# Crossbar transposes amid the loads, and token mixing pair by pair, in a fused sparse attention and MLP mixer

## The chip, the cores and the metric

The kernel runs on one core of one Trainium2 chip. The metric is device time in microseconds, the median over runs. A trace of one execution gives the span, which is 1.6 to 2.1 us shorter than the time of the same execution. PE is the matmul engine, PEld its weight loads, DVE the vector engine, ACT the scalar engine, POOL and SP the engines that here mostly issue DMAs: POOL the loads, SP the stores and the crossbar transposes. Executions of one kernel still differ by an us or two; in the record, those of the kernel before have a mean clock of 0.986 to 1.000, and those at 0.993 are mostly 0.7 to 1.5 us longer.

## The reference

Four batches of eight heads, 768 positions, 64 channels. Attention is masked by blocks of 32 (band, edges, three sampled blocks per row), then a token mixing with a residual and a channel mixing with a residual follow.

```python
scores = scale * np.matmul(q, k.transpose(0, 1, 3, 2))
scores = np.where(mask, scores, -1e9)
attn = softmax(scores);  x = attn @ v                       # to (B, S, H*D)
h = np.maximum(x.transpose(0, 2, 1) @ w_tok1, 0.0) @ w_tok2
u = x + h.transpose(0, 2, 1)
out = u + np.maximum(u @ w_ch1, 0.0) @ w_ch2
```

## The kernel before

Heads go in 16 pairs, nine steps each. A step is a block of scores on PE, its exp on ACT, from pair 4 on its masking on DVE, and its product with the values (PV) on PE. Before that, DVE lays a pair's keys and queries out anew (the relayout), and they are transposed: on PE with an evacuation (a copy of PE's result to where it is used), or by a DMA, the crossbar. A planner inside the kernel simulates the engines and decides, when the kernel is built, in which order each engine gets its instructions. On the chip every engine keeps the order it was given, and stands (waits with its next instruction) where the plan was wrong. What matters here:

```python
def landing(issue, nbytes):                     # the plan's idea of when a load lands
    dma["free"] = max(dma["free"], issue + 3.2 * US) + nbytes / RATE      # RATE = 200
    return Ev(dma["free"] + 0.15 * US)

def relayout(p):                                # DVE: loaded keys, queries -> order for the transpose
    ...
        lay = sbw.tile([128, NC, 2, D], BF16, tag=f"{nm}lay", bufs=2, name=f"{nm}lay{p}")
        nc.vector.tensor_copy(out=lay[...], in_=raw.rearrange("p h c d -> p c h d"))
    ...
    if nm != "v" and p >= 3:
        deps.append(qT_there[p - 2, 1])         # two buffers: the transpose of p-2 has read them
    if nm != "v" and p >= NPE:
        deps.append(all_loaded)                 # not before all loads are there

def crossbar(p):                                # pairs p >= NPE (8): transposed by DMA
    nc.sync.dma_start_transpose(out=bufs[p % NV][:, 0, :]..., in_=lays[nm]...)
    deps = [lays[nm + "ev"], mask_there, qk_done[p - NV]]
    ev = P.op(("sp",), {"sp": 900.0}, deps, emit, prio=1, lat=5000.0)     # planned landing: 5 us
```

Pairs below NPE are transposed on PE, 12 matmuls a pair, and evacuated by DVE or ACT. From pair 4 on the exps are masked on DVE by a multiplication ("cut"), scores run on 64 rows at a time, two steps per visit, and PE fills with channel mixing.

The softmax here doesn't subtract the row's maximum and nothing guards it: scores larger than these inputs give would overflow.

Of the kernel before, what the change touches and what calls it, by code (L numbers as in the profile page):

```python
# [8 lines left out]
FP32 = mybir.dt.float32  # L9
BF16 = mybir.dt.bfloat16  # L10
# [40 lines left out]
class Planner:  # L51
# [21 lines left out]
    def stream(self, prio, gen):  # L73
        self.streams.append([prio, self.count, gen, None])
        self.count += 1
        self.streams.sort(key=lambda s: (s[0], s[1]))
# [27 lines left out]
    def step(self):  # L104
# [3 lines left out]
        if self.free_at["pe"] <= self.now:  # L108
            for s in self.streams:
# [65 lines left out]
def kernel(  # L175
# [23 lines left out]
    NPE = 8  # L199
# [24 lines left out]
    RATE = 200.0  # L224

    def landing(issue, nbytes):
        dma["free"] = max(dma["free"], issue + 3.2 * US) + nbytes / RATE
        return Ev(dma["free"] + 0.15 * US)
# [62 lines left out]
    def first(eng, nm, src, hf):  # L291
        eng.dma_start(
            out=f32[nm][:, :, 3 * hf : 3 * hf + 3, :],
            in_=APx(src, 3 * hf * D, [[NC * D, 128], [S * D, 2], [1, 3 * D]]),
        )

    nc.sync.dma_start(out=samp64[R, :], in_=sampled_blocks)
    first(nc.scalar, "q", q, 0)
    first(nc.sync, "k", k, 0)
    first(nc.sync, "k", k, 1)  # L300
    first(nc.sync, "q", q, 1)

# [12 lines left out]
    def idle_mm():  # L315
        nc.tensor.matmul(
            out=idle_ps[:, 0, :], lhsT=free(one[:, 0:1], 0, [[0, 128]]),
            rhs=free(one[:, 0:1], 0, [[0, 512]]), start=True, stop=True,
        )

    for i in range(8):
        idle_mm()
# [17 lines left out]
    load_pair(2, 6.4 * US, 2)  # L340
    load_tok(8.7 * US)
    load_pair(3, 10.2 * US, 3)
# [26 lines left out]
    nc.vector.tensor_copy(out=sampf[R, :], in_=samp64[R, :].bitcast(I32))  # L369
# [10 lines left out]
    nc.vector.tensor_copy(out=ktb[0][R, 1, 0:384], in_=indf[:, 0:384])  # L380
# [5 lines left out]
    def first_lay(copy, nm, hf):  # L386
        copy(
            out=lay0[nm][:, 3 * hf : 3 * hf + 3, :, :],
            in_=f32[nm][:, :, 3 * hf : 3 * hf + 3, :].rearrange("p h c d -> p c h d"),
        )  # L390

    def first_turn(nm, hf):
        t = psM.tile([128, 3, 128], BF16, tag="pm", name=f"t{nm}first{hf}")
        for c in range(3):
            nc.tensor.matmul(
                out=t[:, c, :], lhsT=lay0[nm][:, 3 * hf + c, :, :].rearrange("p h d -> p (h d)"),
                rhs=ident[:, :], start=(c == 0), stop=(c == 2), is_transpose=True,
            )
        return t

    def first_evac(copy, nm, hf, hd, t):
        buf = (ktb if nm == "k" else qtb)[0]
        copy(
            out=buf[0:64, hd, 384 * hf : 384 * hf + 384],
            in_=t[64 * hd : 64 * hd + 64, :, :].rearrange("p c s -> p (c s)"),
        )

    def e2_mm(hf, pool, tag):
        t = pool.tile([128, 512], FP32, tag=tag, name=f"pm_e2_{hf}")
        nc.tensor.matmul(  # L410
            out=t[R, 0:384], lhsT=t2add[R, :], rhs=indf[:, 384 * hf : 384 * hf + 384],
            start=True, stop=True,
        )
        return t

    def e2_copy(copy, hf, hd, t):
        copy(out=qtb[0][R, hd, 384 * hf : 384 * hf + 384], in_=t[R, 0:384])

    vcopy, acopy = nc.vector.tensor_copy, nc.scalar.copy
    first_lay(acopy, "q", 0)  # L420
    qt0 = first_turn("q", 0)
    first_lay(acopy, "k", 0)
    kt0 = first_turn("k", 0)
    e2a, e2b = e2_mm(0, psM, "pm"), e2_mm(0, psO, "po")
    for i in range(4):
        idle_mm()
    first_evac(acopy, "q", 0, 0, qt0)
    first_evac(acopy, "q", 0, 1, qt0)
    e2_copy(acopy, 0, 0, e2a)
    first_evac(vcopy, "k", 0, 0, kt0)  # L430
    first_evac(vcopy, "k", 0, 1, kt0)
    e2_copy(vcopy, 0, 1, e2b)
    first_lay(acopy, "k", 1)
    first_lay(vcopy, "q", 1)
    START = 6.3 * US
# [3 lines left out]
    P.free_at["dve"] = START + 550.0  # L439
    f_there = {("k", 0): Ev(START), ("q", 0): Ev(START), ("k", 1): Ev(), ("q", 1): Ev()}  # L440

# [3 lines left out]

    def first_rest():

        def band(eng):
            nc.vector.tensor_copy(out=ktb[0][R, 1, 384:S], in_=indf[:, 384:S])

        P.op(("dve",), {"dve": 250.0}, [], band, prio=0)
        for nm in ("k", "q"):
            box, last, rel = {}, Ev(), Ev()

            def emit(nm=nm, box=box, rel=rel):
                P.take("pm", rel)
                box["t"] = first_turn(nm, 1)

            yield 330.0, [Ev(START + (200.0 if nm == "k" else 600.0))], [("pm", 1)], emit, last
            for hd in range(2):  # L460
                def evac(eng, nm=nm, hd=hd, box=box):
                    first_evac(vcopy, nm, 1, hd, box["t"])

                ev = P.op(("dve",), {"dve": 350.0}, [last], evac, prio=0)
                f_there[nm, 1].same_as = ev
                rel.same_as = ev
        box, last, rel = {}, Ev(), Ev()

        def emit():
            P.take("pm", rel)  # L470
            box["t"] = e2_mm(1, psM, "pm")

        yield 330.0, [], [("pm", 1)], emit, last
        for hd in range(2):
            def copy(eng, hd=hd, box=box):
                e2_copy(vcopy, 1, hd, box["t"])

            e2_there = P.op(("dve",), {"dve": 555.0}, [last], copy, prio=0)
            rel.same_as = e2_there
        rows_there[0] = e2_there  # L480
        built.add(("row", 0))
        for n in range(1, NV):
            def spread(eng, n=n):
# [6 lines left out]
                ("dve",) if n == 1 else ("sp",), {"dve": 560.0, "sp": 800.0}, [e2_there], spread,  # L490
# [10 lines left out]
    def mask_stream():  # L501
# [13 lines left out]
        yield 330.0, [rows_there[0]], [("pm", 1)], emit, last  # L515
# [36 lines left out]
    all_loaded = Ev()  # L552

    def relayout(p):
        lays = {}
        for nm in ("k", "q", "v") if p else ("v",):
# [18 lines left out]
            if nm != "v" and p >= NPE:  # L575
                deps.append(all_loaded)
            lays[nm + "ev"] = P.op(("dve",), {"dve": 320.0}, deps, emit, prio=2 if nm != "v" else 3)
# [4 lines left out]
    def crossbar(p):  # L582

        lays = relayout(p)
        for nm, bufs, there in (("k", ktb, kT_there), ("q", qtb, qT_there)):
# [6 lines left out]
            ev = P.op(("sp",), {"sp": 900.0}, deps, emit, prio=1, lat=5000.0)  # L592
            there[p, 0], there[p, 1] = ev, ev

    def transposes(p):
# [4 lines left out]
        if p == 0:  # L600
# [3 lines left out]
            for hd in range(2):  # L604
                kT_there[p, hd], qT_there[p, hd] = f_there["k", 1], f_there["q", 1]
# [5 lines left out]
        for nm, bufs, there in (("k", ktb, kT_there), ("q", qtb, qT_there)):  # L611
# [29 lines left out]
            for hd in range(2):  # L641
# [7 lines left out]
                ev = P.op(("dve", "act"), {"dve": 550.0, "act": 740.0}, [last], evac, prio=2)  # L649
# [4 lines left out]
    def alias(a, b):  # L654
        a.same_as = b

# [3 lines left out]
    xs, x_there, po_of = {}, {}, {}  # L660
# [43 lines left out]
    def qk_deps(p, t, jj):  # L704
# [3 lines left out]
        deps = [f_there["k", int(jj > 0)], f_there["q", int(t > 0)]]  # L708
        return deps + [rows_there[0]] * (t > 0)

    def qk_stream():
        todo = list(steps)
        while todo:
            s = todo.pop(0)
            p, t, jj = s
            yield lambda p=p: (p, 1) in qT_there
# [10 lines left out]
            s2 = todo.pop(0)  # L727
            yield lambda p=s2[0]: (p, 1) in qT_there
            evs = [Ev(), Ev()], [Ev(), Ev()]

            def emit(s=s, s2=s2, evs=evs):
                scores(s, evs[0][0], evs[1][0])
                scores(s2, evs[0][1], evs[1][1])
                evs[0][0].t = P.now + 330.0 + P.PE_LAT + P.SEM
                evs[0][1].t = P.now + 560.0 + P.PE_LAT + P.SEM

            yield 650.0, qk_deps(*s) + qk_deps(*s2), [("ps", 2), ("et", 2)], emit, None
            for x, ev in zip((s, s2), evs[0]):
                if x[1:] == (2, 2):
                    alias(qk_done[x[0]], ev)  # L740
# [56 lines left out]
    st = {}  # L797
# [32 lines left out]
    def tok(b, g):  # L830
        deps = [x_there[2 * g + 4 * b + i, h] for i in range(2) for h in range(3)] + [tok1_there]

        urgent = 0.5 if b == 0 else 3
# [20 lines left out]
        a_there = relu_op(lambda: a_t[:, :, :], box["pm"][:, :, :], [last], urgent)  # L854
        alias(rel, a_there)
        u_evs = []
        for s2 in range(3):
# [22 lines left out]
            ev = P.op(("dve",), {"dve": 695.0}, [last], add, prio=urgent)  # L880
# [3 lines left out]
        if b > 0:  # L884
            turn_by_crossbar(b, g, u_evs)
            return
        for dmc in (2 * g, 2 * g + 1):
            last, rel, tbox = Ev(), Ev(), {}
            for sc in range(NC):
                def emit(sc=sc, dmc=dmc, rel=rel, tbox=tbox):  # L890
                    if sc == 0:
                        if dmc == 0:
                            new_uT(b)
                        P.take("pm", rel)
                        tbox["pt"] = psM.tile([128, NC, 128], BF16, tag="pm", name=f"pm_ut_{b}_{dmc}")
                    nc.tensor.matmul(
                        out=tbox["pt"][:, sc, :],
                        lhsT=st[b]["u"][:, g, sc, 128 * (dmc % 2) : 128 * (dmc % 2) + 128],
                        rhs=ident[:, :], start=(sc == 0), stop=(sc == NC - 1), is_transpose=True,
                    )  # L900
                tags = [("pm", 1)] if sc == 0 else []
                if sc == 0 and dmc == 0:
                    tags.append(("uT", 1))
                yield 56.0, [u_evs[sc // 2]], tags, emit, last if sc == NC - 1 else None

            def evac(eng, dmc=dmc, tbox=tbox):
# [187 lines left out]
```

## Time and profile before

257.33 us, median of 4 runs (256.97 of the first 3). How to read the page: its first block gives busy us per engine, its second one digit per fortieth of the span.

| | before |
|---|---|
| span of the trace | 255.4 us |
| first score / start of channel mixing / end of last matmul | 6.46 / 54.44 / 252.20 us |
| crossbar transposes: first one, landing | 72.5 us, 2.8 us |
| TensorE clock | full in all slices |

### The profile page before, as it was taken

Reading aid. Unit: us, or ns where it says so; the run is one execution under the profiler, and the core shown is the slowest. Engines: PE = TensorE matmul, PEld = TensorE weight load, DVE = VectorE, ACT = ScalarE, POOL = GpSimd, SP = SyncE. Lnnn points to the kernel's source line nnn. Section 1 sums busy time; section 2 is a strip of 40 time slices with the busy share of each in tenths; the row PEclk is TensorE's granted clock in tenths of the full one; section 3 lists DMA queues with packets and bytes.
Section 4 is the critical chain, followed back from the end, with each engine's and each line's share of the span. In section 5 each row is a group of like instructions: output and inputs, shape, how many; then the busy total and the mean of one; then the engine's idle time right before and its main releaser. Section 6 shows DMA issues by size and latency. Waiting matters only on the chain.

```text
span 255.4 us, 6578 instructions
## 1 busy us (share of the span) xinstructions
PE 248.7 (97%) x2757; PEld 158.6 (62%) x2757; DVE 180.4 (71%) x397; ACT 174.1 (68%) x215; POOL 49.7 (19%) x84
## 2 busy tenths in 40 slices
PE   8899999999999999999999999999999999999995
PEld 3578888766576556656676566557567744566444
DVE  7788678899899889798989898988986313200222
ACT  5889999988878667678888777767776420277100
POOL 8745979477400000000000000000000000000000
PEclk9999999999999999999999999999999999999999
DMA  6999999999975533194034311411500222300122
GB/s 148 175 217 200 212 204 205 204 201 201 203 129 112 76 102 88 41 168 105 0 51 76 64 41 20 129 41 44 78 27 4 39 66 83 123 0 3 41 109 96
DMA packets 42462, 26.35 MB, mean 103 GB/s; under 512 B 23681, under 2 KB 38801, under 8 KB 42433
## 3 DMA queue, kind: packets, MB, share of 16 engines
q0 software_dynamic: 15104, 12.98, 32.2%
q1 hardware_dynamic: 27056, 12.76, 21.0%
q8 instruction: 21, 0.34, 0.5%
q10 hardware_dynamic: 272, 0.20, 0.3%
q14 instruction: 9, 0.07, 0.1%
HBM read 26.74 MB, written 6.29 MB: 129 GB/s over the span
## 4 chain that ended last, share of the span: by engine, by line
PE 77%; DMA 18%; POOL 2%; issue 1%; DVE 1%; POOLq 0%
PE pm_ch L960 25%; PE pm_ch L934 25%; PE po L762 11%; PE ps L676 10%; DMA w_ch<-in_moe_w_ch_dram 8%; DMA qraw<-in_q_dram 7%; PE pm_tok L867 3%; PE pm_tok L842 3%; DMA vraw<-in_v_dram 3%; POOL vraw L254 1%; POOL kraw L254 1%; POOL ktb L330 0%; POOL ktb L326 0%; POOL qraw L254 0%; DVE x L875 0%
## 5 line engine op out<-in xcount | busy, mean ns | idle before, releaser
L686 ACT ACTIVATE et<-ps 128x1024 bf16<-128x1024 f32 x144 | 139.1, 1024 | 33.6 <-PE ps L676 33.0
L934 PE MATMUL pm_ch<-uT,w_ch 128*128 128x384 bf16 x384 | 73.3, 326 | 0.1
L960 PE MATMUL pm_ch<-w_ch,rc 128*128 128x512 bf16 (+2 forms) x312 | 71.3, 363 | 0.0
L694 DVE TENSOR_TENSOR et<-et,mask 128x1024 bf16<-128x1024 bf16 x108 | 69.9, 684 | 1.7 <-ACT et L686 1.7
L762 PEld LDWEIGHTS <-et 128*128 128x128 bf16 x1152 | 48.4, 97 | 18.2 <-issue 2.1
L676 PE MATMUL ps<-qtb,ktb 64*128 64x256 bf16 (+1 forms) x576 | 54.7, 272 | 1.3 <-ACT et L686 0.9
L762 PE MATMUL po<-vaug,et 128*128 128x65 bf16 x1152 | 54.9, 193 | 0.4 <-DVE x L777 0.4
L934 PEld LDWEIGHTS <-w_ch 128*128 128x128 bf16 x384 | 34.0, 97 | 21.0 <-issue 3.1
L972 DVE TENSOR_TENSOR o<-pm_ch,x 128x512 f32<-128x512 f32 x23 | 15.8, 687 | 41.0 <-PE pm_ch L960 41.0
L804 ACT ACTIVATE rc<-pm_ch 128x384 bf16<-128x384 f32 x56 | 27.6, 492 | 24.9 <-PE pm_ch L934 24.6
L676 PEld LDWEIGHTS <-ktb 64*128 64x128 bf16 (+1 forms) x576 | 29.3, 95 | 20.5 <-issue 15.7
L960 PEld LDWEIGHTS <-rc 128*128 128x128 bf16 x312 | 26.9, 98 | 24.1 <-issue 2.5
L806 DVE TENSOR_SCALAR rc<-pm_ch 128x384 bf16<-128x384 f32 x40 | 22.0, 555 | 5.7 <-PE pm_ch L934 5.0
L777 DVE TENSOR_TENSOR x<-po,recip 128x256 bf16<-128x256 f32 x48 | 20.4, 424 | 1.7
L875 DVE TENSOR_TENSOR x<-pm_tok,x 128x512 bf16<-128x512 f32 x24 | 15.9, 686 | 2.7 <-PE pm_tok L867 2.6
L776 DVE RECIPROCAL recip<-po 128x4 f32<-128x4 f32 x48 | 8.7, 180 | 12.6 <-PE po L762 12.0
L867 PE MATMUL pm_tok<-a_t,w_tok 128*128 128x256 bf16 x96 | 13.5, 275 | 0.1
L842 PE MATMUL pm_tok<-x,w_tok 128*128 128x256 bf16 x96 | 12.5, 273 | 0.0
L867 PEld LDWEIGHTS <-w_tok 128*128 128x128 bf16 x96 | 10.3, 127 | 1.6 <-issue 0.8
L842 PEld LDWEIGHTS <-w_tok 128*128 128x128 bf16 x96 | 8.9, 98 | 1.9 <-issue 0.8
L254 POOL DMA_DIRECT2D vraw<-in_v_dram x10 | 7.4, 738 | 3.0 <-DVE et L694 1.4
L532 POOL COPY mask<-maskb 128x240 bf16<-128x240 bf16 (+1 forms) x18 | 7.7, 505 | 0.0
(96 smaller groups left out, 114.4 us busy)
## 6 DMA issues: line engine op xcount, KB each, us to landing
out_dram<-o SPq DMA_DIRECT2D x23, 256.0 KB, 2.2
w_ch<-in_moe_w_ch_dram POOLq DMA_DIRECT2D x8, 384.0 KB, 10.0
vraw<-in_v_dram POOLq DMA_DIRECT2D x10, 192.0 KB, 7.8
kraw<-in_k_dram POOLq DMA_DIRECT2D x9, 192.0 KB, 8.8
qraw<-in_q_dram POOLq DMA_DIRECT2D x9, 192.0 KB, 8.0
w_tok<-in_moe_w_tok_dram POOLq DMA_DIRECT2D x2, 384.0 KB, 10.4
ktb<-in_v_dram POOLq DMA_DIRECT2D x3, 192.0 KB, 7.3
kf<-in_k_dram SPq DMA_DIRECT2D x2, 192.0 KB, 3.4
```

The source lines that it names most:

```text
L676: nc.tensor.matmul(out=ps[:, hd, 256 * i : 256 * i + 256], lhsT=ktb[n][rows, h, 256 * jj + 128 * i : 256 * jj + 128 * i + 128], rhs=qtb[n] ...
L686: nc.scalar.activation(out=et[:, :, :], in_=ps[:, :, :], func=AF.Exp, scale=0.125)
L694: nc.vector.tensor_tensor(out=ets[s][:, :, :].rearrange("k h (i q) -> k h i q", i=2), in0=ets[s][:, :, :].rearrange("k h (i q) -> k h i q" ...
L762: nc.tensor.matmul(out=po[:, hd, c, :], lhsT=et[:, hd, 256 * i + 128 * c : 256 * i + 128 * c + 128], rhs=va[:, hd, 2 * jj + i, 0:65], star ...
L777: nc.vector.tensor_tensor(out=free(xs[b][:, pb // 2, 2 * t, 128 * (pb % 2) : 128 * (pb % 2) + 128], 0, [[64, 2], [256, 2], [1, 64]],), in0 ...
L804: nc.scalar.activation(out=o(), in_=i, func=AF.Relu)
L806: nc.vector.tensor_scalar(out=o(), in0=i, scalar1=0.0, scalar2=None, op0=ALU.max)
L842: nc.tensor.matmul(out=box["pm"][:, t, :], lhsT=w_tok1[:, sc, 128 * t : 128 * t + 128], rhs=xs[b][:, g, sc, :], start=(t == 0 and sc == 0) ...
L867: nc.tensor.matmul(out=ubox["pm"][:, i, :], lhsT=w_tok2[:, t, :, 2 * s2 + i], rhs=a_t[:, t, :], start=(i == 0 and t == 0), stop=(i == 1 an ...
L875: nc.vector.tensor_tensor(out=st[b]["u"][:, g, 2 * s2 : 2 * s2 + 2, :], in0=ubox["pm"][:, :, :], in1=xs[b][:, g, 2 * s2 : 2 * s2 + 2, :], ...
L934: nc.tensor.matmul(out=pbox["pm"][:, 0:384], lhsT=w_ch1[:, dmc, 128 * cc : 128 * cc + 128], rhs=st[b]["uT"][:, dmc // 2, 3 * sh : 3 * sh + ...
L960: nc.tensor.matmul(out=pbox["pm"][:, 0:n], lhsT=box["rc"][:, cc, 128 * sc : 128 * sc + 128], rhs=w_ch2[:, cc, lo : lo + n], start=(cc == 0 ...
```

## The change

The intent: take the transposes of pairs 5 to 7 off PE, spread the token mixing of batch 0 under the exps, and start the first pair sooner. The core of the diff, cut:

```diff
-    NPE = 8
+    NPE = 5
...
-    RATE = 200.0
+    RATE, SHARED = 200.0, 150.0
...
+        rate = RATE if dma["free"] < 28 * US else SHARED
...
-            if nm != "v" and p >= NPE:
-                deps.append(all_loaded)
-            lays[nm + "ev"] = P.op(("dve",), {"dve": 320.0}, deps, emit, prio=2 if nm != "v" else 3)
+            lays[nm + "ev"] = P.op(("dve",), {"dve": 320.0}, deps, emit, prio=0.1 if p == 0 else 3 if nm == "v" else 0.6 if p < NT0 else 2)
...
-            ev = P.op(("sp",), {"sp": 900.0}, deps, emit, prio=1, lat=5000.0)
+            ev = P.op(("sp",), {"sp": 1200.0}, deps, emit, prio=1, lat=9000.0)
...
+    def mixing():
+        return 0 in st and all(e.t is not None and e.t < P.now for e in st[0]["uT_there"])
...  # scores of pairs >= 4 go one step a visit until mixing(), two after
-    P.stream(0.5, tok_stream((0,)))
-    P.stream(3, tok_stream((1, 2, 3)))
+    P.stream(1.7, first_tok_stream((0, 1, 2)))     # tok_pair(p): 128 columns, one pair
+    P.stream(0.5, first_tok_stream((3,)))
+    P.stream(3, tok_stream())
```

Besides (cut here): the first pair is loaded, turned and copied in pieces of two chunks instead of three; idle matmuls fill PE between them; one part of POOL's time goes to a relayout; one of the last stores is issued by ACT; some priorities of the plan differ; and in the plan channel mixing starts only when all of its inputs are there.

## The prediction

> **What bounds the kernel now.** I read the page first, for the engines over the whole span. PE is full from the third slice to the end; ACT is full only in slices 3 to 7 (about 13 to 45 us).
>
> ```profile
> span 255.4 us, 6578 instructions
> PE 248.7 (97%) x2757; PEld 158.6 (62%) x2757; DVE 180.4 (71%) x397; ACT 174.1 (68%) x215; POOL 49.7 (19%) x84
> ...
> PE   8899999999999999999999999999999999999995
> ...
> ACT  5889999988878667678888777767776420277100
> ...
> DMA  6999999999975533194034311411500222300122
> ```
>
> The clock row is 9 in every slice, so PE is bound by what it is given, in order. A full PE can still wait, so I then cut the span at events found in the timeline and asked for each stretch: first score at 6.46, first exp of the second half at 16.51, first score of pair 4 at 43.8, start of channel mixing proper at 54.44, last matmul's end near 252.2.
>
> ```profile
> 6.46:16.51 10.05, 8.67 (x112) 6.04 (x111) 8.54 (x22) 8.35 (x9) 7.26 (x11) 1.00 1.18 193
> 16.51:43.85 27.34, 26.87 (x424) 23.61 (x424) 20.32 (x53) 26.45 (x29) 21.02 (x38) 1.00 1.23 205
> 43.85:54.44 10.59, 10.12 (x161) 7.75 (x160) 9.63 (x22) 9.81 (x12) 6.25 (x10) 1.00 1.28 203
> 54.44:200.80 146.36, 146.22 (x1757) 91.49 (x1756) 127.04 (x267) 110.52 (x130) 9.67 (x14) 1.00 0.44 83
> ```
>
> The columns after the length are busy us of PE, weight loads, DVE, ACT, POOL, then clock, DMA share and GB/s. Up to 43.85 the exps set the pace (ACT 26.45 of 27.34); from 54.44 PE is full (146.22 of 146.36) and what is queued on it simply adds up. Between them the score pairs alternate with transposes and batch 0's token mixing on PE. The timeline of ACT shows the pace: one exp each 0.942 us back to back, and only about two exps per 2.5 us after 44.
>
> ```profile
> 13.21 2.86 ACT L686 ACTIVATE et<-ps 128x1024 bf16<-128x1024 f32 x3 [0.63 <-PE ps L676]
> 16.51 9.42 ACT L686 ACTIVATE et<-ps 128x1024 bf16<-128x1024 f32 x10 [0.43 <-PE ps L676]
> 24.90 10.39 ACT L686 ACTIVATE et<-ps 128x1024 bf16<-128x1024 f32 x11
> ...
> 46.91 2.01 ACT L686 ACTIVATE et<-ps 128x1024 bf16<-128x1024 f32 x2
> ```
>
> So the span is T + R: T is when channel mixing begins (54.44), R the PE work queued behind it plus the tail (255.4 - 54.44 = 201.0). The change can only move T, and whatever it leaves undone at T is added to R.
>
> **What the Trainium skill says.** "TensorE: Matmul & The Clock Gate", Part 2 (What happens when you issue a matmul), says back-to-back matmuls cost their column count, with drain hidden. The trace agrees: 128 columns 56 ns, 256 columns 109 ns, 384 columns 162 ns start to start. "TensorEngine Tiling (Array Packing)", Key Properties, says a change of tiling mode drains TensorE. From pair 4 on, scores use 64 rows at a time; around each such visit of 8 the trace has some 95 ns extra before and a last matmul longer by 135 ns, so a visit of two steps costs 0.54 + 0.10 = 0.64 us. I estimate a visit of one step at 0.42. "DMA: Bandwidth & Descriptors", DMA Transpose (X-bar), lets a transpose run beside ordinary DMAs; before has none amid the loads (first at 72.5), so what it costs there no run shows yet.
>
> **The change part by part.**
> (a) Crossbar for pairs 5 to 7. Gone from PE: 3 pairs x 12 x 56 ns = 2.0 us, and 6 evacuations of 0.55 us on DVE or ACT. All of this stood between 39 and 46 us, before T. Six more transposes on the DMA queues cost PE nothing if they land in time. Pair 5's landings are at 27.7, 28.3 and 29.3; its relayouts stand in DVE's new order at about exp 31, near 37 us; two issues of 1.3 us and a landing I put at 6 us (2.8 on an empty queue) give 46, and its first score is wanted after T. Pairs 6 and 7 have more slack. So no gain or loss beyond PE's.
> (b) Token mixing by pair: 96 matmuls of 128 columns (5.4 us) for 48 of 256 (5.2): +0.1. It spreads the work under the exps of pairs 1 to 4, where PE has room, instead of at 46 to 54.
> (c) Single visits until batch 0 is mixed: pair 4 becomes single steps. 10 singles for 5 pairs: 10 x 0.42 - 5 x 0.64 = +1.0 us of PE, 8 of them before T where ACT is the limit.
> (d) First pair in two-chunk pieces: DVE's copies are 256 columns instead of 384. First score about 0.3 us sooner (6.46 to 6.15): the table of allowed blocks is ready at about 5.05 as now, evacuations shrink from 0.37 to about 0.28 and the row copy from 0.56 to about 0.42. Fillers and the last store's queue: nothing.
>
> At T the new order has issued 44 scores, not 46, and 5 fewer groups of 8 PV matmuls; no channel matmul has been taken early, 2 were before. Behind T it has then 49 pair visits (as before) + 2 singles (0.84) + 5 x 0.24 (1.2) + 2 x 0.16 (0.3) = 2.35 us more. R = 201.0 + 2.35 = 203.3.
>
> T itself: the 44th score needs a score buffer, so 42 exps must be over. First exp at about 6.75; with no wait at all T = 6.75 + 42 x 0.942 = 46.3. But I followed the new DVE order against landings that the trace of before records, since the load queue keeps its order. The one that matters is the query of pair 2:
>
> ```profile
> 7.10 7.65 DMA qraw<-in_q_dram
> ```
>
> (chain of waits: issued 7.10, landed 14.75). In the new order DVE lays out keys and queries of pair 2 ahead of three of the four evacuations of pair 1. So: relayout ends 14.75 + 0.35 = 15.1; three evacuations of 0.55 end at 16.75; pair 1's first score at 16.8, its exp (the tenth) at 17.4. Before, that exp began at 16.51 + 0.94 = 17.45. All that the faster start won is thus waited away here. Then token matmuls of pair 0 wait for the first token weight (landed 18.61): 0.4 us. Pair 3's key and query (21.04, 22.02) and the one PV bank cost some 0.15 + 0.1 + 0.3 us by the same walk, up to exp 21. After that I find ACT continuous; I allow 0.3 more. T = 17.4 + 33 x 0.942 + 1.25 = 49.8.
>
> Span = 49.8 + 203.3 = 253.1, 2.3 less than 255.4. I take that off the median of 256.97: 254.7 us.
>
> **Rivals.**
> First, ACT unbroken from the start: if the loads land as the plan thinks (query of pair 2 a microsecond earlier) pair 1 follows pair 0 at once, T is near 47, span 250.3, time 251.9 or 2% faster. For it: the plan was evidently made to get this. Against it: the loads run at a steady 0.98 us per tensor and 200 GB/s in the page's rate row, already full, and the new order puts a POOL copy before that very load.
> Second, transposes amid full queues come late, and PE, in order, stands at pair 5's first score. DMA is at 9 until 68 us; a landing of 14 us instead of 6 would put that score at 54 and cost about 3 us: 257.5. Against it: pair 5 is asked for some 9 us after its transposes would be done at the unloaded speed.
> Third, DVE becomes the bound before T. I add up its rows to T: 35 us of work in the 42 us from 6.75; after 24.6 some 20 us in 24. It keeps up, but cuts of pair 4 are postponed behind the token additions, and a backlog at T could cost PE up to 1 us: 255.7.
> Fourth, PE idles hidden by ACT: all that leaves PE before T was not on the path; then T moves only by exps. This is largely what I assume.
>
> **Range and chances.** The only large unknown is T. 47.4 gives 252.3 and 51.4 gives 256.3; a little for a second surprise: 252.0 to 256.5. Over 2% faster needs below 251.83, T below 47, so nearly no wait: 0.12. Over 2% slower needs a stall of 7 us: 0.02.
>
> **What would show it.** In the changed trace: first score about 6.15; tenth exp near 17.4 with an ACT gap of 1 to 2 us before it, released by PE's scores, themselves by DVE's evacuation behind the relayout of pair 2's query; 0.942 us per exp from there; channel mixing starting at 49.8 with pair 4 in visits of four; 203.3 from there to the end; PE full after T. The prediction is wrong if the gap before the tenth exp is missing (then faster), if pair 5's first score waits for a DMA, or if PE loses more than before behind T.

## More of the kernel before

The prediction shows the lines. One more matters for later: the transposes' landing, from the view of DMA issues (count, median us from issue to landing).

```profile
kraw<-in_k_dram POOLq DMA_DIRECT2D x9, 192.0 KB, 8.8
qtb<-qlay SPq DMA_TRANSPOSE x8, 2.8
```

## The result, and the profile after

264.96 us, median of 4 runs (264.51 to 266.78): 3.1% slower, ratio 1.0307 (95%: 1.025 to 1.0364). The prediction said 254.7, range 252.0 to 256.5. It was wrong, and in the direction to which it gave 0.02.

From the page of the changed kernel:

```profile
span 262.7 us, 6638 instructions
...
PE   8979999969789999999999999999999999999995
...
ACT  6989999917648866877878877677787430177100
...
PEclk9999999979979999999999999999999999999999
DMA  5999999999999443265406031521030053210123
```

Two slices, 8 and 11 counted from 0 (53 to 59 and 72 to 79 us), have a granted clock of about 0.7 and PE is not full in slices 8, 10 and 11. In the profile before, neither occurred. The stretches around them, same columns as in the prediction's table:

```profile
50.39:52.66 2.27, 2.27 (x23) 0.98 (x21) 1.35 (x3) 2.06 (x4) 0.72 (x1) 1.00 1.26 192
52.66:55.34 2.68, 0.17 (x3) 0.01 (x1) 1.02 (x3) 1.18 (x2) 1.44 (x3) 1.00 1.28 191
55.34:59.21 3.87, 3.87 (x32) 2.09 (x32) 3.12 (x7) 0.04 (x1) 2.14 (x3) 0.56 1.28 191
59.21:70.25 11.04, 11.04 (x122) 6.55 (x118) 7.29 (x17) 8.54 (x11) 5.25 (x8) 1.00 1.31 179
70.25:73.08 2.83, 0.18 (x2) 0.00 (x0) 1.75 (x5) 1.03 (x2) 1.53 (x3) 0.96 1.29 195
73.08:76.27 3.19, 3.19 (x24) 1.91 (x24) 1.79 (x4) 0.98 (x2) 1.23 (x3) 0.50 1.40 145
```

Channel mixing begins at 50.39, where the prediction had 49.8. Then PE stands for 2.7 us, runs at half clock for 3.41 us (the record in the trace; 0.56 is the mean of the stretch), stands again for 2.8 us and again has 3.41 us at half clock. What it stands behind is seen on DVE and PE, from the timeline (start, length, instruction, and in brackets the idle time before it and what ended it):

```profile
51.19 0.55 DVE L619 COPY klay<-kf 128x768 bf16<-128x768 bf16 x1
54.32 0.36 DVE L619 COPY qlay<-kf 128x768 bf16<-128x768 bf16 x1 [2.58 <-DMA qtb<-qlay]
54.60 1.29 DVE L753 TENSOR_TENSOR et<-et,mask 128x1024 bf16<-128x1024 bf16 x2
...
71.33 0.36 DVE L619 COPY qlay<-ktb 128x768 bf16<-128x768 bf16 x1 [3.19 <-DMA qtb<-qlay]
```

```profile
55.34 0.42 PE L824 MATMUL po<-vaug,et 128*128 128x65 bf16 x8 [2.51 <-DVE et L753]
...
73.08 0.62 PE L824 MATMUL po<-vaug,et 128*128 128x65 bf16 x8 [2.65 <-DVE et L753]
```

The copy at 54.32 lays out the query of pair 7. It did not wait for that query, which had landed at 41.2. It waited for a transpose to finish. There are two buffers for relaid queries, and pair 7's is the one from which the crossbar was still reading pair 5's. The chain of waits names that transpose, issued at 41.11:

```profile
41.11 13.12 DMA qtb<-qlay
```

It took 13.1 us, where the plan has 9 and an undisturbed one takes 2.8. The copy at 71.33 is pair 9's, and waited in the same way for pair 7's. Behind the stuck copy, in DVE's order, stand the mask multiplications; behind them the PV matmuls; behind those, in PE's order, the channel mixing that had all it needed. The view of DMA issues shows that loads and transposes slow one another (8.8 us to landing for a key load before, 2.8 for a query transpose):

```profile
kraw<-in_k_dram POOLq DMA_DIRECT2D x9, 192.0 KB, 10.6
qtb<-qlay SPq DMA_TRANSPOSE x11, 6.0
```

Run 2 below, which has all of the change but the early transposes, has 8.2 and 2.8. The transposes whose landing the trace records while loads run took 9.2 to 14.8 us, one more 15.5 by the chain of waits; the later ones 2.8. What in the DMA makes them late was not asked; SP's own instruction for one took 1.5 to 7.2 us between 39 and 71 us, and mostly 1.2 later.

The account: from the start of channel mixing to the end the prediction had 203.3 us; measured 262.7 - 50.4 = 212.3. The 9.0 us are two stands (2.7 + 2.8) and two windows of 3.41 us in which PE did half its work (1.7 each, an estimate that run 12 tests): 8.9 us.

### The profile page after: what moved, and what is told of

The parts are those of the page before. It is cut to its first block, busy times and chain, and to the rows that moved or that the text cites. A ratio compares the mean times of both kernels' runs of the same rounds, so it can differ in the third digit from the quotient of the medians.

```text
span 262.7 us, 6638 instructions
## 1 busy us (share of the span) xinstructions
PE 248.7 (95%) x2763; PEld 158.8 (60%) x2784; DVE 178.3 (68%) x396; ACT 174.9 (67%) x220; POOL 50.9 (19%) x85
## 4 chain that ended last, share of the span: by engine, by line
PE 77%; DMA 15%; POOL 3%; DVE 3%; issue 1%; DVEq 0%
PE pm_ch L1068 23%; PE pm_ch L1041 21%; PE ps L735 12%; PE po L824 12%; DMA qtb<-qlay 11%; DMA kraw<-in_k_dram 4%; PE pm_tok L926 3%; PE pm_tok L901 3%; POOL vraw L258 1%; DVE x L839 1%; POOL kraw L258 1%; PE pm_tok_p L961 1%; POOL qraw L258 1%; DVE qlay L619 0%; PE pm_tok_p L984 0%
## 5 line engine op out<-in xcount | busy, mean ns | idle before, releaser
L1041 PE MATMUL pm_ch<-uT,w_ch 128*128 128x384 bf16 x384 | 75.6, 333 | 0.0
L1068 PE MATMUL pm_ch<-w_ch,rc 128*128 128x512 bf16 (+2 forms) x291 | 66.7, 362 | 1.0 <-issue 0.2
L735 PE MATMUL ps<-qtb,ktb 64*128 64x256 bf16 (+1 forms) x576 | 56.2, 273 | 0.9 <-DVE qtb L699 0.2
L865 ACT ACTIVATE rc<-pm_ch 128x384 bf16<-128x384 f32 x62 | 30.6, 493 | 28.8 <-PE pm_ch L1041 28.5
L867 DVE TENSOR_SCALAR rc<-pm_ch 128x384 bf16<-128x384 f32 x34 | 18.7, 554 | 5.2 <-PE pm_ch L1041 4.6
L934 DVE TENSOR_TENSOR x<-pm_tok,x 128x512 bf16<-128x512 f32 x18 | 11.8, 686 | 3.6 <-PE pm_tok L926 3.4
L926 PE MATMUL pm_tok<-a_t,w_tok 128*128 128x256 bf16 x72 | 10.6, 277 | 0.0
L901 PE MATMUL pm_tok<-x,w_tok 128*128 128x256 bf16 x72 | 10.1, 272 | 0.0
L926 PEld LDWEIGHTS <-w_tok 128*128 128x128 bf16 x72 | 7.5, 128 | 1.3 <-issue 1.1
L258 POOL DMA_DIRECT2D kraw<-in_k_dram x9 | 6.6, 735 | 7.2 <-DVE uT L1018 3.3
## 6 DMA issues: line engine op xcount, KB each, us to landing
out_dram<-o SPq DMA_DIRECT2D x23, 256.0 KB, 2.0
kraw<-in_k_dram POOLq DMA_DIRECT2D x9, 192.0 KB, 10.6
ktb<-in_v_dram POOLq DMA_DIRECT2D x3, 192.0 KB, 10.6
```

Source lines behind the costliest of these rows:

```text
L258: nc.gpsimd.dma_start(out=raw, in_=APx(src, 2 * p * S * D, [[NC * D, 128], [S * D, 2], [1, NC * D]]),)
L735: nc.tensor.matmul(out=ps[:, hd, 256 * i : 256 * i + 256], lhsT=ktb[n][rows, h, 256 * jj + 128 * i : 256 * jj + 128 * i + 128], rhs=qtb[n] ...
L865: nc.scalar.activation(out=o(), in_=i, func=AF.Relu)
L867: nc.vector.tensor_scalar(out=o(), in0=i, scalar1=0.0, scalar2=None, op0=ALU.max)
L901: nc.tensor.matmul(out=box["pm"][:, t, :], lhsT=w_tok1[:, sc, 128 * t : 128 * t + 128], rhs=xs[b][:, g, sc, :], start=(t == 0 and sc == 0) ...
L926: nc.tensor.matmul(out=ubox["pm"][:, i, :], lhsT=w_tok2[:, t, :, 2 * s2 + i], rhs=a_t[:, t, :], start=(i == 0 and t == 0), stop=(i == 1 an ...
```

## The experiments

All are of 4 runs with a profile and 3 rounds against the kernel before. Two theories at the start. A: the stuck relayout (a buffer held by a late transpose) is the whole loss, the clock a consequence. B: the transposes are too late as such, and any order will stand somewhere. C, a rival for the clock alone: PE is throttled for its own load.

**1. A third buffer for relaid keys and queries.** Memory was full, so the last stores' own buffers went.

```diff
-tag=f"{nm}lay", bufs=2
+tag=f"{nm}lay", bufs=3
-o = sbw.tile([128, 256], FP32, tag="olast", bufs=3, ...)
+o = sbw.tile([128, DM], FP32, tag="o", bufs=3, ...)
```

> The changed kernel with a third buffer for the relaid keys and queries (memory taken from the last stores' buffers); the order of instructions on all engines is unchanged. Theory A (the relayout of pair 7's query waits for the buffer that the late crossbar transpose of pair 5 still reads; VectorE, PE and then the clock stand behind it): the waits of 2.6 and 3.2 us on VectorE and PE's gaps of 2.7 and 2.8 us vanish, the clock row stays at 9, channel mixing begins at 50.4 as in the changed kernel, span near 50.4 + 203.3 = 253.7, time about 255.5, that is 0.99 of before. Rival B (the transposes are late as such): PE stands at pair 5's first score instead, the span falls by under 3 us, to 260 or more. Rival C (PE is throttled for its own load, waits apart): the clock still falls to 0.7 in one or two slices.

Measured 258.32 us (257.14 to 259.29), ratio 1.0032 (0.9991 to 1.0072); span 257.6. The order of instructions is the same on all engines, both stands of PE are gone, and of the waits for transposes 1.1 us are left on DVE (0.9 and 0.2), which hold up nothing on PE. So 7 of the 7.6 us of loss come back. The relayout of pair 7's query now starts at once:

```profile
53.76 0.34 DVE L619 COPY qlay<-kf 128x768 bf16<-128x768 bf16 x1
```

That is theory A; B falls for this order (in run 6 it comes back). From the start of channel mixing (52.59) to the end it is 205.0 us; 1.1 of the 1.7 over my 203.3 is the end, where the last store now waits for a buffer. The late start of the mixing is this:

```profile
PEclk9995999999999999999999999999999999999999
```

```profile
15.00:18.41 3.41, 1.97 (x23) 1.40 (x22) 2.53 (x5) 3.28 (x5) 0.71 (x1) 1.00 1.11 218
18.41:25.24 6.83, 6.83 (x64) 5.59 (x64) 3.79 (x11) 3.45 (x5) 3.88 (x7) 0.50 1.31 201
```

The profile is of the slowest of the four executions (mean clock 0.986; the others 0.990 to 0.999). In it the clock fell early, after a window in which PE was busy 1.97 of 3.41 us. The gap there is a wait for the token weight, 1.2 us. The changed kernel has the same gap; in its profile the clock did not fall there. So C falls too (the later windows stayed full at the same load), and the early waits of the changed order go with a slow window in some executions.

**2. No crossbar amid the loads.** NPE = 8 and the wait for all loads back, everything else of the change kept.

> The changed kernel with pairs 5 to 7 back on PE and all crossbar transposes after the last load, all else of the change kept. Theory A and rival B both: no gap over 1 us on PE after 50 us, clock at 9, tensors land every 0.98 us until 74 us. Channel mixing begins at 51 to 53 (2 us more of PE work before it, part of it under the exps), span 254 to 256.5, time 256 to 258: about as before. If it were the pairwise token mixing or the single visits that cost the time, it would stay near 262 us of span.

Measured 258.34 us (257.61 to 260.74), ratio 1.0051 (0.9997 to 1.0105); span 255.9, clock full. Channel mixing begins at 51.26. The time was just over the range I gave; the trace has one stand of 1.0 us at 111 us. Pairwise mixing and single visits do not make the loss: without the early transposes the change is as fast as before.

**3. The crossbar part alone, on the kernel before.**

```diff
-    NPE = 8
+    NPE = 5
-            if nm != "v" and p >= NPE:
-                deps.append(all_loaded)
```

> The kernel before with one part of the change alone: crossbar transposes from the sixth pair on, relayouts no longer held until all loads are planned to have landed; plan constants as before (landing of a transpose 5 us). Theory A and B: transposes land after 10 us or more, VectorE waits for a transpose before a relayout for 2 us or more at least twice, PE gaps follow, the clock falls to 0.7 in one or two slices; span 259 to 266, so slower than before by 1.5 to 4%. If the rest of the change is at fault instead: within 1% of before.

Measured 275.91 us, ratio 1.0708 (1.0671 to 1.0745): worse than I allowed, as this plan thinks that a transpose lands in 5 us. From the list of waits (total, times, longest) and the page:

```profile
DVE klay L565 <- DMA ktb<-klay: 10.0, 3, 5.6
```

```profile
PEclk9899999857599999999999999999999999999999
```

So this part by itself costs 18 us with the old plan constants. That it costs less within the change I put down to the longer planned landing there; run 4 fits that, but it was not tried alone.

**4. A planned landing of 15 us** instead of 9, in the changed kernel, so that the relayouts come later in the order.

```diff
-lat=9000.0
+lat=15000.0
```

> The changed kernel with the planned landing of a transpose set to 15 us (9 in the change), so that the order places the relayouts of pairs 7 and later behind more of the mask multiplications. Theory A: with the plan near the measured 11 to 15 us, VectorE's waits for transposes fall from 6.5 us in all to under 2, PE's two long gaps go, the clock stays at 9, span 253 to 256. Rival B: PE waits at pair 5's or 6's first score for the transpose instead and the span stays over 259.

Measured 259.47 us, ratio 1.0067 (1.0027 to 1.0107); span 257.9, a little over what I gave. One stand of 2.0 us stays, at 63 us, where DVE waits 2.4 us with the relayout of pair 8's query. The list of waits puts that down to a load, but the chain of waits names the transpose of pair 6's query, the earlier holder of the buffer:

```profile
47.68 16.59 DMA qtb<-qlay
```

The chain is right: with the counts that the kernel, built again, waits for, the semaphore of pair 8's own load was there at 54.9 in the trace, and the transpose's last update came at 64.27, just before the relayout at 64.36. So this is the same wait once more, at a landing of 16.6 us. In this profile too the clock fell early (3.41 us from 19.84). The order alone, with two buffers, thus takes most of the loss away, and what stays is again the buffer.

**5. A third buffer for queries alone**, the stores left whole.

```diff
-tag=f"{nm}lay", bufs=2
+tag=f"{nm}lay", bufs=3 if nm == "q" else 2
-tag="olast", bufs=3            # three of 256 columns
+tag=f"olast{n}", bufs=256 // n # one of 256, two of 128
```

> The changed kernel with a third buffer for the relaid queries alone, and the last stores keep three buffers of their own (cut to the sizes they need), since the first experiment's sharing of them cost 1.4 us at the end; order of instructions unchanged. Theory A (query buffer): VectorE's waits for a transpose gone or under 1 us in all, PE has no gap over 1 us after 50 us and no slow clock there, the end after the last matmul is 3.2 us again. From the start of channel mixing to the end 203.5 to 204.5 us. Channel mixing begins at 50.4 where the clock stays full before it, at 52 to 53 where it falls early as in the first and fourth experiments; time 255.5 to 258. If the key's buffer holds too, a wait for a key transpose of over 1 us appears.

Measured 261.42 us, ratio 1.0131 (1.0056 to 1.0206): a miss. The first stand is gone; the second remains (2.9 us at 67.5, half clock from 71.7), now behind the relayout of a key. The list of waits puts that wait down to a load; the chain of waits has the transpose of pair 7's key there, issued at 54.63 and landed 13.8 us later, 0.09 us before the relayout of pair 9's key. A later wait, of 1.1 us, is put down to a key transpose at once. With both third buffers (run 1) neither is there. So the key's buffer holds too, as the last sentence of the expectation allowed.

**6. The plan's landings set to the measured ones**, on top of 5.

```diff
-    dma = {"free": 7.6 * US}
+    dma = {"free": 8.0 * US}
-        rate = RATE if dma["free"] < 28 * US else SHARED
+        rate = 180.0 if dma["free"] < 20 * US else RATE if dma["free"] < 38 * US else SHARED
```

> As e5_q3, and the plan's landings of the first loads set to what the trace shows (stream from 8.0 us, 180 GB/s until 20 us, 200 until 38, 150 after). Theory: the early waits (1.3 us for the token weight, 1.6 us before the tenth exp, 0.5 and more for relayouts of pairs 2 and 3) are the plan's early landings and put the clock at risk; with the order made for true landings PE has no gap over 0.6 us between 12 and 40 us, no half clock there in any profile, tenth exp at about 16.5 to 17, channel mixing at 49 to 50; span 252.5 to 254, time 254 to 256, below before by 0.5 to 1.2%. Rival: the loads themselves limit, and the waits only move: channel mixing again at 50.4 or later.

Measured 266.66 us, ratio 1.0324 (1.0259 to 1.0388): a bad miss, and instructive. The wait for the token weight is gone, but channel mixing begins at 51.03 all the same, so the rival was right: the early waits only moved. And the new order runs into the key transposes harder than any earlier order of the changed kernel, since the transposes' planned landing was still 9 us:

```profile
79.00 0.36 DVE L619 COPY klay<-kraw 128x768 bf16<-128x768 bf16 x1 [5.78 <-DMA ktb<-klay]
```

```profile
80.75 0.62 PE L824 MATMUL po<-vaug,et 128*128 128x65 bf16 x8 [4.96 <-DVE et L753]
```

Before that, at 57.18, PE stood 1.9 us at pair 5's first score for the transpose of its query: here the place that theory B and the prediction's second rival named does cost time.

**7. The same with 13 us for a transpose.**

```diff
-lat=9000.0
+lat=13000.0
```

> As e6_q3_land with the planned landing of a transpose at 13 us, near the measured 11 to 15. Theory: nothing waits for a transpose any more, but with the buffer's wait already gone this gains under 1 us; span within 1 us of e6_q3_land. If late landings still cost something there, this one is faster by more.

Measured 256.24 us (256.0 to 256.52), ratio 0.9923 (0.9863 to 0.9982). My theory said under 1 us of gain over run 6; it gained 10. No wait for a transpose is listed, PE has no gap over 1 us, and channel mixing begins at 50.97 with 203.7 us to the end, near the prediction's sum. It is faster than both kernels; than the one before by 0.8% here and 0.5% in run 9. The one constant lets the planner change the order in many places.

```profile
55.00:60.00 5.00, 5.00 (x57) 3.09 (x55) 3.01 (x8) 3.15 (x7) 2.26 (x4) 1.00 1.36 158
60.00:70.00 10.00, 10.00 (x115) 6.09 (x113) 9.45 (x19) 8.38 (x11) 4.88 (x7) 1.00 1.35 179
70.00:80.00 10.00, 10.00 (x131) 6.91 (x130) 8.55 (x22) 8.90 (x12) 2.90 (x4) 1.00 1.27 191
```

The transposes still take 9 to 14 us here; nobody asks before.

**8. The same landings of the first loads without crossbar amid the loads**, two query buffers.

> The changed kernel without crossbar transposes amid the loads (pairs 5 to 7 on PE, two query buffers) and with the landings of e6_q3_land (200 GB/s to the end, as nothing shares the queues). What the crossbar part is worth when it makes no stall is the difference to e6_q3_land: I expect channel mixing at 51 against 49.5, span 254 to 255, so 1 to 1.5 us slower than e6_q3_land and about 0.5% faster than before. If it is as fast as e6_q3_land, the transposes on PE were hidden under the exps all along.

Measured 258.04 us, ratio 1.0016 (0.9931 to 1.01); span 255.9, against 254.6 of run 7, channel mixing at 50.73 with 44 scores issued, against 45 in run 7. Taking the transposes off PE is therefore worth 1.3 us of span when nothing waits for them (1.8 us by the medians of the time). That is the size I expected, though against run 6, which had stands of its own; and the start of channel mixing does not show it: the gain is in what PE has left after it.

**9. A third key buffer on top of 7** (two full store buffers for three).

```diff
-bufs=3 if nm == "q" else 2
+bufs=3
-tag="o", bufs=3
+tag="o", bufs=2
```

> As e7_q3_land_lat13 with a third key buffer too (two full store buffers for three); same order. In that run nothing waited for a transpose, so the theory is: no change, span 254 to 255.5, time within 0.4% of it. If it is faster by over 1 us, waits for the key's buffer were still hidden in it.

Measured 256.25 us (256.0 to 256.26), ratio 0.9954 (0.9928 to 0.998). As expected: with the right landing in the plan, more buffers add nothing. It also confirms run 7 in other rounds.

**10. Pair 4's scores in visits of two again**, on 7.

```diff
-            if todo and (...) and mixing():
+            if todo and (...):
```

> As e7_q3_land_lat13, with pair 4's scores visited two steps at a time again (the single visits of the change undone). My prediction charged single visits 1.0 us of PE, mostly under the exps: so 0 to 1 us faster, span 253.6 to 254.8. If single visits matter for keeping the exps fed, channel mixing begins later and the span is 1 us or more longer.

Measured 260.26 us, ratio 1.0119 (1.0084 to 1.0154): 4.0 us slower than run 7, where I had 0 to 1 faster. Channel mixing begins at 50.15, but with 42 scores issued instead of 45, so more is left behind it, and the trace shows more small waits on mask multiplications up to 117 us, and waits of 2.9 us for key transposes. The order changed in many places; how much of the 4 us is due to the visits themselves is open.

**11. Batch 0's token mixing as before the change**, on 7 (the old function put back, so no short diff).

> As e7_q3_land_lat13, with batch 0's token mixing as it was before the change (by two pairs, 256 columns). If the pairwise mixing is what brought channel mixing forward by 3 to 4 us, it begins at 53 to 54 here with 46 or 47 scores issued; less work is left behind it, so span 255.5 to 257. If the crossbar transposes brought it forward, channel mixing begins at 51 and the span equals that of e7_q3_land_lat13.

Measured 261.49 us, ratio 1.0164 (1.0136 to 1.0192). Channel mixing begins at 57.67 with 47 scores issued. Part of it is a stand of 1.7 us at 41 and half clock from 44.3, so this order was again unlucky, and the size (5.3 us) is not the pairwise mixing's alone. That the crossbar brought channel mixing forward is not what it shows: with the crossbar and without pairwise mixing it begins later than before the change.

**12. Idle matmuls ahead of the stands**, in the changed kernel: 20 of 252 columns before two PV groups. (The fillers of a new bank must open their own accumulation.)

> The changed kernel as it is, with 20 idle matmuls of 252 columns (2.1 us) given to PE just ahead of the two PV groups at which it stood for 2.7 and 2.8 us. Theory (each stand also costs half a slow window of 3.41 us, 1.7 us): PE stands 0.6 us instead, the clock stays at 9, span 262.7 - 2 x 1.7 = 259.3. If the clock falls for another reason, or its fall costs little, the span stays at 262 or more.

Measured 265.2 us, ratio 1.03 (1.0253 to 1.0348); span 263.5. At the first place it did what theory says:

```profile
52.91 2.37 PE L822 MATMUL po<-one 128*128 128x252 bf16 x20
55.40 0.42 PE L830 MATMUL po<-vaug,et 128*128 128x65 bf16 x8
```

PE's records leave 0.1 us before the PV group instead of 2.5, and the clock stays full. From that group's start to the second visit of scores after it there are now 4.65 us instead of 6.26 (60.05 - 55.40; 61.60 - 55.34): 1.6 us for the clock alone, where I had estimated 1.7. The second set I had put one group too early: it ran at 66.9, cost its 2.2 us, and the stand at 71.5 came as ever, with half clock after it. So the span missed the 259.3 that I gave. Minus 1.6, plus 2.2, plus 0.2 for a later start of channel mixing (50.63) is the 0.8 by which it is longer than the changed kernel's.

## Why the prediction was wrong

**T was right, in part by luck.** "T = 17.4 + 33 x 0.942 + 1.25 = 49.8": measured 50.39. The walk held at its end: the 42nd exp was over at 49.98, and the 44th score came at 50.06. Its terms missed on both sides. The first score came at 5.76 (predicted 6.15). The tenth exp came at 16.78 (17.4), since pair 2's query was laid out at 14.01, where the sum had it land at 14.75. The order is as argued, three of pair 1's evacuations behind that relayout:

```profile
14.01 0.34 DVE L619 COPY qlay<-qraw 128x768 bf16<-128x768 bf16 x1
14.38 0.56 DVE L699 COPY ktb<-tk 64x768 bf16<-64x768 bf16 x1
14.97 1.14 DVE L699 COPY qtb<-tq 64x768 bf16<-64x768 bf16 x2
```

```profile
13.01 3.19 ACT L745 ACTIVATE et<-ps 128x1024 bf16<-128x1024 f32 x3 [0.30 <-PE ps L735]
16.10 0.78 ACT L697 COPY ktb<-tk 64x768 bf16<-64x768 bf16 x1
16.78 1.93 ACT L745 ACTIVATE et<-ps 128x1024 bf16<-128x1024 f32 x2
19.58 8.98 ACT L745 ACTIVATE et<-ps 128x1024 bf16<-128x1024 f32 x9 [0.87 <-PE ps L735]
```

But the exps paused 0.6 us before the tenth, with an evacuation in the pause, and not the 1 to 2 us of the prediction. From there to T it took 1.2 us more than in the sum: the token weight's wait was 1.2 us on PE rather than 0.4, and ACT was not continuous (it also waited 0.5 us at 29). Three small slips change nothing: 0.942 is a row's length through its count, while from start to start the same row has 0.93; ACT's 9s stand at 19 to 51 us and not at 13 to 45; and the second rival's 3 us would make 257.7.

**R was wrong, and the step that failed is in (a).** It reads "two issues of 1.3 us and a landing I put at 6 us (2.8 on an empty queue)" and concludes "So no gain or loss beyond PE's". Two errors are in it. The size: 10.8 and 13.1 us for pair 5, not 6 (and 1.6 and 2.3 us for the issues). And the place: I asked only when pair 5's scores want the transposed tiles. I did not ask who waits for the tile that the transpose reads. That buffer comes free at the landing, and the relayout of pair 7 wants it at 51.7, in an engine that keeps its order. The line that says so, two buffers and the dependence on the transpose of p-2, is in the code shown above. The second rival had the landing (14 us) but put the wait on the scores and so charged 3 us; the third had DVE as the place but for its load. Of the prediction's three signs of being wrong, the last came true: PE lost more than before behind T. With the stands removed the sum 201.0 + 2.35 = 203.3 holds: run 1, which has the same order and 44 scores at T, has 205.0 with 1.1 of it at the stores. The 203.7 of run 7 are near it in part by luck, as its order differs.

**The clock was not in the sum at all.** I read its row of 9s as a constant of the kernel. In these traces it goes with PE's stands: where PE was kept busy instead (run 12) it stayed full, and a fall after a stand of 2.7 us cost 1.6 more.

**(b), (c), (d).** With the crossbar back (run 2) the rest is level with before, and with measured landings (run 8) too. (c)'s size of a single visit held: 0.32 us from its start to the next instruction (43.91 to 44.23) and 0.10 before it. That undoing single visits gains was not confirmed: it lost time (run 10), for reasons not settled.

**What the Trainium skill was used for.** Column counts and the mode switch held: the visits of four and of eight have the same 95 ns before them in the changed trace. The 135 ns depend on what follows: the last matmul's record is 203 ns before a PV group and 337 before channel mixing. That a transpose may run beside ordinary DMAs is said on the page that the prediction names, but in its section Rules for kernel authors. "TensorE: Matmul & The Clock Gate", Part 1 (What's actually happening), which I had not used, states a half clock after an idle window of about 3.4 us: the traces agree in the length of the slow stretches (3.41 us or multiples of it) and in the factor (0.5), not in the need for a whole idle window (below).

## What to carry to other kernels

When a copy is moved from an engine to a DMA, ask two things of its landing: who wants what it writes, and who wants back what it reads. In a kernel with a planned order, take the landing from a trace under the load that will be there, since an order made for a landing that is 4 us too early does not lose 4 us once but can lose at each reuse of the buffer (2.3 and 5.8 us on DVE in run 6); here changing that one number from 9 to 13 us was worth 10 us (runs 6 and 7). And a long stand of PE is to be charged with the slow clock after it: here every one of 2.5 us or more had one, and it cost 1.6 us where that could be measured.

## What the Trainium skill lacked or had wrong

- "DMA: Bandwidth & Descriptors", Rules for kernel authors, says that a transpose next to ordinary DMAs needs nothing. It says so of correctness, and the runs agree: their outputs were correct. What no page has is the time: 9 to 15.5 us to landing beside full load queues in the changed kernel (16.6 in run 4) against 2.8 alone, and key loads of 10.6 us against 8.2 without early transposes (run 2).
- "TensorE: Matmul & The Clock Gate", HAM oscillation, warns of idle gaps over about 3.4 us. Here shorter ones had half clock after them: all nine gaps of 2.5 us or more in the profiles between 8 and 200 us came with a slow window. Of those of 1.1 to 1.9 us, three did (1.22 in run 1, 1.16 in run 4, 1.56 in run 11) and five did not (1.18 in the changed kernel, 1.87 in run 4, 1.10 in run 5, 1.21 and 1.92 in run 6).
- A slow stretch begins and ends on a raster of 3.41 us (in the changed kernel at 55.80 and 72.86, five times 3.41 apart), but PE's busy share of the 3.41 us before does not settle whether it comes: 1.97 us busy was followed by one in run 1, 2.02 at the same place in the changed kernel was not; in run 3, 2.57 was and 1.84 was not. What decides stays open, and the same page has no figure for it.
